# Attention and two expert layers on one core: for 24 pairs of heads the products with values are made two pairs at a time

## The chip, the cores and the metric

The kernel runs on one core of a Trainium2 chip. The metric is the device time of one execution in microseconds (us). Besides the DMA queues the core has five engines that run side by side, each through its own instructions in program order: TensorE (PE in the profile; PEld is its loading of stationary operands), VectorE (DVE), ScalarE (ACT), GpSimd (POOL) and SyncE (SP), which here issues nearly all DMAs.

## The reference, cut to what matters

```python
scores = scale * np.matmul(q, k.transpose(0, 1, 3, 2))        # (2, 8, 576, 576), head_dim 64
kth = np.partition(scores, -32, axis=-1)[..., -32:-31]
scores = np.where(scores >= kth, scores, -1e9)
attn = np.exp(scores - scores.max(-1, keepdims=True))
attn = attn / (attn.sum(-1, keepdims=True) + 1e-09)
attn_out = np.matmul(attn, v)                                 # then (1152, 512), heads side by side
out = sum(p[:, e:e+1] * (relu(x @ w1[e]) @ w2[e]) for e in range(4))      # w1 (4, 512, 1024)
return np.maximum(np.maximum(out @ m1, out @ m2), out @ m3) @ m_out        # 512 -> 768 -> 512
```

## The kernel before, in words

The 1152 rows are cut into 9 tiles of 128 and the 8 heads into 4 pairs, so there are 36 units of attention, numbered n = 0 to 35; the code calls such a unit a `Pair` (128 rows, two heads). Tile 4 (`MIXED`) has 64 rows of either batch; its units are n = 16, 18, 20 and 21. The program is written slot by slot: unit n begins at slot 8n, and tables (`LOOSE`, `BOTH`, `THIRD`) say at which slot each of its steps is emitted. For the units spoken of here these steps are, counted from slot 8n:

- -4 and 0: `scores` (two heads j), TensorE into two PSUM banks each (L418, L423), ScalarE copies to `s` (L430). `s` of head 0 has a ring of 5 buffers, of head 1 one of 4.
- 0 to 11: `topk`, VectorE takes the largest 8 four times (L443) and strikes them out (L445); then ScalarE or VectorE make the masked exponentials `p` with their sums (L457 to L471).
- 14: `trans_p`, TensorE turns `p` (four 128x128 blocks of each head, L489, and one of the two ends, L494) and ScalarE copies to `pt` (L492, L497). 14 and 15: `guard` (L502), `recip` on VectorE (L508), 16: `spread` on ScalarE, `rb` (L512), one buffer.
- 17: `pv`, the products with values into one bank `psv`: the block diagonal `v_last` over the full array (L531, two instructions for each such product), then for four row blocks and two heads a product over half of the array's columns (L534, 16 instructions; a unit of tile 4 does both parts for either batch in turn). 17: `trans_r`, TensorE turns `rb` (L517), ScalarE copies to `r` two slots later (L519).
- 20 and 21: `norm` on VectorE (L541, `psv` times `r`), `split_x`: ScalarE rounds to `xh` (L554), GpSimd takes the rest `xl` (L555).

Between the slots a planner emits products of the expert layers (L680 to L682 in three terms of a split product, L765 to L842 for unsplit ones) until the charged TensorE time (`pe(...)`) reaches that charged to VectorE (`dve(...)`). Their weights come over SP into `raw` (L212, 5 buffers), ScalarE rounds them (`whi`, L271), GpSimd or VectorE take the rest (`wlo`, L277); ScalarE applies Relu to a finished bank (`h`, L822) and VectorE takes the rest (L824). After unit 35 only the products and the conversion of the second layer's 64-bit weights are left (`wide_load` L222 into the buffers of `s`).

`v` has five buffers and `v_last` six for the eight pieces (batch, pair of heads); the load of piece (1, 2), L345 and L349, is emitted one slot behind the products of unit 19, and takes the buffer of `v` that unit 18 reads last.

Of the kernel before, what the change touches and what calls it, by code (L numbers as in the profile page):

```python
# [10 lines left out]
F32 = mybir.dt.float32  # L11
# [3 lines left out]
AF = mybir.ActivationFunctionType  # L15
ALU = mybir.AluOpType
# [12 lines left out]
S1 = 4  # L29
# [15 lines left out]
LOOSE = dict(stag=4, new=1, scores=-4, at=(14, 14), pv=17, rec=15, lag=2, sum=0)  # L45

EARLY = 7

ALONE_FROM, ALONE_STEP = -8, 4
LOAD, LOAD_FULL = 11, 9  # L50
SHARE, AHEAD = (1.0, 1.0, 1.0), 6
AHEAD_S = 5
# [8 lines left out]
def kernel(  # L61
# [14 lines left out]
    nc = tc.nc  # L76
    B, HP, D, _, S = k.shape
    NT, DM = out.shape
    E = gates.shape[2]
    P = 128  # L80
# [3 lines left out]
    NR = S // P  # L84
    TAIL = S - NR * P
# [5 lines left out]
    MIXED = 4  # L91
# [17 lines left out]
    const = ctx.enter_context(tc.tile_pool(name="const", bufs=1))  # L109
    kv = ctx.enter_context(tc.tile_pool(name="kv", bufs=2))  # L110
    qp = ctx.enter_context(tc.tile_pool(name="qp", bufs=2))
    at = ctx.enter_context(tc.tile_pool(name="at", bufs=2))
# [7 lines left out]
    ident = const.tile([P, P], F32, name="ident")  # L120
# [12 lines left out]
    def pe(n):  # L133
        clock["pe"] += n / 2400.0

    def bank(name):
        return pg.tile([P, 512], F32, tag="g", name=name)
# [169 lines left out]
    kraw, kT, vt, qraw, qT = {}, {}, {}, {}, {}  # L307
# [11 lines left out]
            nc.sync.dma_start(out=kfull[rows(n), heads], in_=k[0, hp][:, heads])  # L319
            between()  # L320

    v_last = [const.tile([P, P], F32, name="v_last%d" % i) for i in range(6)]
    for x in v_last:
        nc.gpsimd.memset(x, 0.0)

# [71 lines left out]
    class Pair:  # L397
        def __init__(self, n):
            self.n = n
            self.c, self.hp, self.t = pairs[n]  # L400
            self.s, self.w, self.m, self.nb = {}, {}, {}, {}
            self.p = self.rs = None
            self.pt = {}

            self.did = set()

            self.on_pool = [n in ON_POOL[j] for j in range(2)]
            self.on_act = [n in ON_ACT[j] for j in range(2)]
# [74 lines left out]
        def trans_p(self, part):  # L483
            assert {("p", j) for j in range(2) if part in (j, 2)} <= self.did
            ps = bank("psp")
            pe(260 * (NR if part < 2 else 1))
            if part < 2:
                for r in range(NR):
                    nc.tensor.transpose(ps[:, r * P:(r + 1) * P], self.p[:, part, part * TAIL + r * P:part * TAIL + (r + 1) * P], ident)  # L489
                d = at.tile([P, NR, P], F32, tag="pt%d" % part, bufs=1, name="pt")  # L490
                self.pt[part] = d
                return lambda: [nc.scalar.activation(out=d, in_=ps.rearrange("p (r n) -> p r n", r=NR), func=AF.Copy),  # L492
                                self.did.add(("pt", part))]
            nc.tensor.transpose(ps[:, 0:P], self.p.rearrange("p j s -> p (j s)")[:, NR * P:NR * P + 2 * TAIL], ident)  # L494
            d = at.tile([P, P], F32, tag="pt2", name="pt4")
            self.pt[2] = d
            return lambda: [nc.scalar.activation(out=d, in_=ps[:, 0:P], func=AF.Copy), self.did.add(("pt", 2))]  # L497
# [10 lines left out]
            nc.vector.reciprocal(out=self.rr, in_=self.rs)  # L508

        def spread(self):  # L510
            self.rb = at.tile([P, 2, D], F32, tag="rb", bufs=1, name="rb")
            nc.scalar.activation(out=self.rb, in_=self.rr.unsqueeze(2).to_broadcast([P, 2, D]), func=AF.Copy)  # L512

        def trans_r(self):
            ps = bank("psr")
            pe(260)
            nc.tensor.transpose(ps[:, 0:P], self.rb.rearrange("p a d -> p (a d)"), ident)  # L517
            self.r = at.tile([P, P], F32, tag="r", name="r")
            return lambda: [nc.scalar.activation(out=self.r, in_=ps[:, 0:P], func=AF.Copy), self.did.add("r")]  # L519

        def pv(self):
            assert {("pt", i) for i in range(3)} <= self.did
            ps = bank("psv")
            pe((NR + 1) * 512)
            if self.t == MIXED:
                parts = [(0, slice(0, TAIL)), (1, slice(TAIL, P))]
            else:
                parts = [(0 if self.t < MIXED else 1, slice(0, P))]
            for b, cols in parts:
                vs, last = vt[b, self.hp]  # L530
                nc.tensor.matmul(ps[:, cols], lhsT=last, rhs=self.pt[2][:, cols], start=True, stop=False)  # L531
                for r in range(NR):
                    for j in range(2):
                        nc.tensor.matmul(ps[j * D:(j + 1) * D, cols], lhsT=vs[:, j * NR + r, :],  # L534
                                         rhs=self.pt[j][:, r, cols], start=False, stop=r == NR - 1)
            self.x = ps

        def norm(self):
            assert "r" in self.did
            self.xt = xfull[:, self.hp, :] if [self.t] in STAGES else at.tile([P, P], F32, tag="xt", bufs=2 + WAITING, name="xt")  # L540
            nc.vector.tensor_tensor(out=self.xt, in0=self.x[:, 0:P], in1=self.r, op=ALU.mult)  # L541

        def split_x(self):
            if not room(self.t):
# [12 lines left out]
    def attention():  # L557

        NP = len(pairs)
        prs = {}  # L560
        later, between = {}, {}

        def options(n):
            return TIGHT if n == HP - 1 else SECOND if n == 2 * HP - 1 else MIDDLE if n in (HP - 2, 2 * HP - 3, 2 * HP - 2) else FIRST if n < 2 * HP else THIRD if n == 3 * HP - 1 else BOTH if n in ON_ACT[1] else LOOSE

        def at_slot(s, f, *a):
            later.setdefault(s, []).append((f, a))
# [3 lines left out]
        for n, (c, hp, t) in enumerate(pairs):  # L571
# [8 lines left out]
            elif n:  # L580
                o = options(max(0, n - 2))
                at_slot(max(8 * n + options(n)["scores"] - LOAD_FULL, 8 * (n - 2) + o["scores"] + o["stag"] + 1), load_full, n)
        free = {"k": -99, "q": -99}
        for key, n in first_use.items():
            if key[0] == "v":
                continue
            s0 = 8 * n
            load, split = (load_k, split_k) if key[0] == "k" else (load_q, split_q)
            at = max(s0 + options(n)["scores"] - (SPLIT_K if key[0] == "k" else SPLIT_Q), free[key[0]] + 2)
            if key[0] == "k" and key[1] and key[2]:  # L590

                at = max(at, 8 * pairs.index((MIXED, key[2] - 1, MIXED)) + options(n)["scores"] + options(n)["stag"] + (1 if key[2] == HP - 1 else 4))
# [3 lines left out]
        for n, (c, hp, t) in enumerate(pairs):  # L596
            s0 = 8 * n
            prs[n] = Pair(n)
            pr = prs[n]
            o = options(n)  # L600

            def two(s, f, *a, lag=o["lag"]):
                at_slot(s, lambda: at_slot(s + lag, f(*a)))
            for j in range(2):
                b0 = s0 + o["stag"] * j
                two(b0 + o["scores"], pr.scores, j, lag=o.get("lag_s", o["lag"]))
                for i in range(7):
                    if o["new"]:
                        later.setdefault(b0 + i, []).insert(0, (pr.topk, (j, i)))
                    else:  # L610
                        at_slot(b0 + i, pr.topk, j, i)
                at_slot(b0 + 2, pr.negate, j)
                at_slot(b0 + 5, pr.exp, j)
                late = o.get("late", MASK_LATE) * pr.on_act[j]
                two(b0 + 7 + late, pr.mask, j, lag=o["sum"] if n < EARLY else 3)
                two(s0 + o["at"][j] if "at" in o else b0 + o["trans"] + late + (late > 0), pr.trans_p, j, lag=o.get("lag_t", o["lag"]))
            two(s0 + o["at"][1] if "at" in o else s0 + o["stag"] + o["trans"], pr.trans_p, 2, lag=o.get("lag_t", o["lag"]))
            at_slot(s0 + o.get("guard", o["rec"] - 1), pr.guard)
            at_slot(s0 + o["rec"], pr.recip)
            at_slot(s0 + o.get("spread", o["rec"] + 1), pr.spread)  # L620
            at_slot(s0 + o["pv"], pr.pv)
            two(s0 + o.get("turn", o["rec"] + 2), pr.trans_r)
            end = max(o["pv"], o["rec"] + 2) + o["lag"]
            if "norm" in o:
                between.setdefault(s0 + o["norm"], []).append((pr.norm, ()))
            else:
                at_slot(s0 + end + 1, pr.norm)
            two(s0 + o.get("split", end + 2), pr.split_x)
        last = {}
        for n, p in enumerate(pairs):  # L630
            o = options(n)
            last[p[0:2]] = 8 * n + o.get("last", max(o["pv"], o["rec"] + 2) + 2 * o["lag"] + 2)
        for n in range(len(alone)):
            at_slot(ALONE_FROM + ALONE_STEP * n, load_alone, n + 1)
        end = max(last.values()) + 1
        s = min(later)
        while s <= end:
            todo = later.pop(s, [])
            i = 0
            while i < len(todo):  # L640
                f, a = todo[i]
# [45 lines left out]
    def begun(ps, wt, xs, N, parts):  # L687

        for f in range(2):
            for a in parts:  # L690

                product(spread(ps[:, f * N:(f + 1) * N], xs[0][a]), [w[:, a, f * P:(f + 1) * P] for w in wt], [x[a] for x in xs], f == a == 0, False)
            yield True
# [386 lines left out]
```

## Time and profile before

| what | us |
|---|---|
| median of 3 runs (lowest, highest) | 752.18 (751.92, 754.55) |
| the profiled execution, its span | 750.64, 748.7 |
| PE busy | 727.5 (97%) |
| PEld busy | 644.9 (86%) |
| DVE busy | 605.3 (81%) |
| ACT busy | 494.1 (66%) |
| POOL busy | 458.2 (61%) |

The span is the time from the first to the last instruction of the profiled execution; 1.94 us of its time lie around it. A matmul is recorded from its start to a modelled end, and matmuls overlap in the array, so what one costs in a stream is read from start to start, not from its duration. The granted clock of TensorE was 1.00 in nearly every stretch.

### The profile page before, as it was taken

The page shows a single profiled execution, that of the slowest core. Times are in us where ns is not written, and L with a number is a line of the kernel's source. Part 1 is how long each engine was busy: PE and PEld are TensorE (multiplying, and loading weights), DVE is VectorE, ACT ScalarE, POOL GpSimd, SP SyncE. Part 2 cuts the span into 40 slices and gives each one's busy share as a digit, 9 for nine tenths or more (in the row PEclk, how much of TensorE's full clock was granted, in tenths as well). Part 3 has the DMA queues.
Part 4 walks back from the last instruction along what each step waited for, and adds up shares of the span by engine and source line. Part 5 has one row for each costly group of instructions (what it writes and reads, how often), then busy time and mean ns, then how long its engine had stood idle before and what let it go on. Part 6 is the DMA issues. An engine that isn't in the chain of part 4 may idle for free.

```text
span 748.7 us, 13553 instructions
## 1 busy us (share of the span) xinstructions
PE 727.5 (97%) x4678; PEld 644.9 (86%) x4678; DVE 605.3 (81%) x1160; ACT 494.1 (66%) x1127; POOL 458.2 (61%) x401
## 2 busy tenths in 40 slices
PE   6899999999999999999999999999999999999998
PEld 3586789888999999898989877999888899999996
DVE  6999989989999899999999958999999643233341
ACT  4668889899987787788796665666555533432531
POOL 2514778689979787697775226678676733442520
PEclk9999999999999999999999999999999999999999
DMA  7684555545637464445433759888688351443501
GB/s 218 185 263 161 154 172 171 154 127 166 188 121 217 114 183 127 146 138 165 132 115 105 281 187 355 248 253 284 222 267 270 135 195 69 157 167 99 196 2 43
DMA packets 56484, 130.14 MB, mean 174 GB/s; under 512 B 9760, under 2 KB 23328, under 8 KB 56416
## 3 DMA queue, kind: packets, MB, share of 16 engines
q1 hardware_dynamic: 48064, 120.69, 51.6%
q10 hardware_dynamic: 8352, 8.59, 3.2%
q8 instruction: 37, 0.61, 0.3%
q14 instruction: 31, 0.25, 0.1%
HBM read 120.60 MB, written 8.65 MB: 173 GB/s over the span
## 4 chain that ended last, share of the span: by engine, by line
PE 65%; DVE 17%; ACT 10%; issue 4%; POOL 3%; DMA 1%; SPq 0%; ACTq 0%; POOLq 0%
PE ps L680 15%; PE ps L682 15%; PE ps L681 15%; DVE m L443 8%; DVE work L445 6%; ACT whi L271 3%; PE psv L534 2%; PE ps L842 2%; POOL wlo L277 2%; PE pss L423 2%; PE psp L489 2%; PE pso L680 2%; PE psa L765 2%; PE pso L681 2%; PE pso L682 2%
## 5 line engine op out<-in xcount | busy, mean ns | idle before, releaser
L277 POOL TENSOR_TENSOR wlo<-raw,whi 128x512 fp32r<-128x512 f32 x228 | 302.9, 1356 | 110.9 <-ACT whi L271 108.3
L271 ACT ACTIVATE whi<-raw 128x1024 fp32r<-128x1024 f32 x148 | 152.6, 1056 | 32.6 <-POOL narrow L248 14.7
L680 PE MATMUL ps<-xl,whi 128*128 128x256 f32 (+1 forms) x520 | 161.0, 310 | 0.3 <-POOL xl L555 0.3
L682 PE MATMUL ps<-xh,wlo 128*128 128x256 f32 (+1 forms) x520 | 157.7, 303 | 0.0
L681 PE MATMUL ps<-xh,whi 128*128 128x256 f32 (+1 forms) x520 | 157.6, 303 | 0.0
L443 DVE MAX8 m<-work 128x8 f32<-128x576 f32 x216 | 155.3, 746 | 0.1
L445 DVE MATCH_REPLACE8 work<-m,work 128x576 f32<-128x576 f32 x144 | 106.9, 743 | 0.0
L680 PEld LDWEIGHTS ps<-xl,whi 128*128 128x128 f32 x520 | 98.6, 190 | 1.7 <-POOL xl L555 0.6
L277 DVE TENSOR_TENSOR wlo<-raw,whi 128x1024 fp32r<-128x1024 f32 x34 | 53.4, 1570 | 56.8 <-ACT whi L271 44.8
L681 PEld LDWEIGHTS ps<-xh,whi 128*128 128x128 f32 x520 | 98.0, 188 | 1.2 <-issue 0.7
L682 PEld LDWEIGHTS ps<-xh,wlo 128*128 128x128 f32 x520 | 97.8, 188 | 0.0
L248 POOL TENSOR_TENSOR narrow<-narrow,raw 128x256 int32<-128x256 int32 x48 | 44.6, 929 | 40.1 <-DVE narrow L245 14.6
L680 PE MATMUL ps<-wlo,h 128*128 128x512 f32 x160 | 65.3, 408 | 0.6 <-POOL wlo L277 0.6
L682 PE MATMUL ps<-whi,h 128*128 128x512 f32 x160 | 63.0, 394 | 1.3 <-POOL h L817 1.3
L681 PE MATMUL ps<-whi,h 128*128 128x512 f32 x160 | 62.7, 392 | 0.0
L430 ACT ACTIVATE s<-pss 128x288 f32<-128x288 f32 x144 | 51.3, 400 | 12.0 <-PE pss L418 11.3
L443 DVE MAX8 m<-s 128x8 f32<-128x576 f32 x72 | 53.9, 748 | 4.0 <-ACT s L430 4.0
L445 DVE MATCH_REPLACE8 work<-m,s 128x576 f32<-128x576 f32 x72 | 53.4, 742 | 0.0
L682 PE MATMUL ps<-x2h,wlo 128*128 128x384 f32 x144 | 48.5, 336 | 0.0
L681 PE MATMUL ps<-x2h,whi 128*128 128x384 f32 x144 | 48.3, 335 | 0.0
L680 PE MATMUL ps<-x2l,whi 128*128 128x384 f32 x144 | 48.2, 335 | 0.0
L947 DVE TENSOR_TENSOR tm<-ps,tm 128x384 f32<-128x384 f32 x36 | 19.9, 555 | 34.1 <-PE ps L682 32.1
(118 smaller groups left out, 1617.7 us busy)
## 6 DMA issues: line engine op xcount, KB each, us to landing
raw<-in_w_dram SPq DMA_DIRECT2D x112, 512.0 KB, 4.2
raw<-narrow SPq DMA_DIRECT2D x36, 512.0 KB, 3.9
whole<-in_w_dram SPq DMA_DIRECT2D x30, 512.0 KB, 5.5
raw<-in_m_dram SPq DMA_DIRECT2D x36, 256.0 KB, 5.1
narrow<-narrow ACTq DMA_DIRECT2D x48, 128.0 KB, 4.5
kraw<-in_k_dram SPq DMA_DIRECT2D x16, 288.0 KB, 4.5
qraw<-in_q_dram SPq DMA_DIRECT2D x48, 64.0 KB, 3.8
raw<-in_mo_dram SPq DMA_DIRECT2D x12, 256.0 KB, 4.1
```

Of the source, the lines that this page charges most:

```text
L248: nc.gpsimd.tensor_tensor(out=out.bitcast(I32), in0=out.bitcast(I32), in1=last, op=ALU.add)
L271: nc.scalar.activation(out=hi, in_=raw, func=AF.Copy)
L277: on.tensor_tensor(out=lo[:, x], in0=raw[:, x], in1=hi[:, x].bitcast(F32), op=ALU.subtract)
L423: nc.tensor.matmul(ps[:, 0:SH], lhsT=l, rhs=r, start=i == 0, stop=i == len(mm) - 1)
L430: nc.scalar.activation(out=s[:, h, :], in_=halves[h][:, 0:SH], func=AF.Copy)
L443: nc.vector.max(m[:, 8 * r:8 * r + 8], src)
L445: nc.vector.match_replace(out=self.w[j], in_to_replace=m[:, 8 * r:8 * r + 8], in_values=src, imm_value=NEG)
L489: nc.tensor.transpose(ps[:, r * P:(r + 1) * P], self.p[:, part, part * TAIL + r * P:part * TAIL + (r + 1) * P], ident)
L680: nc.tensor.matmul(ps, lhsT=lh, rhs=rl, start=first, stop=False)
L681: nc.tensor.matmul(ps, lhsT=lh, rhs=rh, start=False, stop=False)
L682: nc.tensor.matmul(ps, lhsT=ll, rhs=rh, start=False, stop=last)
L947: nc.vector.tensor_tensor(out=tm[:, g], in0=ps, in1=tm[:, g], op=ALU.max)
```

## The change

For twelve units (`HELD`), all even, `pv`, `trans_r`, `norm` and `split_x` are not emitted at their own slots but together with those of the next unit, at that unit's slots: first the block diagonals of both (L531), then all half-array products of both (L534), in two column blocks of one PSUM bank, then both transposes of reciprocals in one bank, two copies to `r`, two `norm`, two `split_x`. All other steps stay at their slots. A held unit's `pt` of the two heads lies in the rings of `s` instead of in the single `pt` buffers; `rb` gets two buffers, `v_last` five instead of six. For a unit of tile 4 both block diagonals come ahead of the half-array products too, held or not.

```diff
+HELD = (8, 12, 14, 16, 18, 22, 24, 26, 28, 30, 32, 34)
-    v_last = [const.tile([P, P], F32, name="v_last%d" % i) for i in range(6)]
+    v_last = [const.tile([P, P], F32, name="v_last%d" % i) for i in range(5)]
...
-                d = at.tile([P, NR, P], F32, tag="pt%d" % part, bufs=1, name="pt")
+                if self.held:
+                    d = at.tile([P, NR, P], F32, tag="s%d" % part, bufs=(AHEAD_S, S1)[part], name="pt")
+                else:
+                    d = at.tile([P, NR, P], F32, tag="pt%d" % part, bufs=1, name="pt")
...
-            self.rb = at.tile([P, 2, D], F32, tag="rb", bufs=1, name="rb")
+            self.rb = at.tile([P, 2, D], F32, tag="rb", name="rb")
...
+        def trans_r(self, *held):
+            both = [*held, self]
             ps = bank("psr")
+            for i, x in enumerate(both):
+                pe(260)
+                nc.tensor.transpose(ps[:, i * P:(i + 1) * P], x.rb.rearrange("p a d -> p (a d)"), ident)
+                x.r = at.tile([P, P], F32, tag="r", name="r")
+            def copy():
+                for i, x in enumerate(both):
+                    nc.scalar.activation(out=x.r, in_=ps[:, i * P:(i + 1) * P], func=AF.Copy)
...
+        def pv(self, *held):
+            both = [*held, self]
             ps = bank("psv")
...
+            pe((NR + 1) * 512 * len(both))
...
+            for i, (x, b, cols) in enumerate(uses):
+                nc.tensor.matmul(x.x[:, cols], lhsT=vt[b, x.hp][1], rhs=x.pt[2][:, cols], start=not i, stop=False)
+            for i, (x, b, cols) in enumerate(uses):
                 for r in range(NR):
                     for j in range(2):
+                        nc.tensor.matmul(x.x[j * D:(j + 1) * D, cols], lhsT=vt[b, x.hp][0][:, j * NR + r, :],
+                                         rhs=x.pt[j][:, r, cols], start=False, stop=i == len(uses) - 1 and r == NR - 1)
...
+            if pr.held:
+                continue
+            both = [prs[n - 1], pr] if n - 1 in HELD else [pr]
+            at_slot(s0 + o["pv"], pr.pv, *both[:-1])
+            two(s0 + o.get("turn", o["rec"] + 2), pr.trans_r, *both[:-1])
             end = max(o["pv"], o["rec"] + 2) + o["lag"]
+            for x in both:
...
+                    at_slot(s0 + end + 1, x.norm)
+                two(s0 + o.get("split", end + 2), x.split_x)
...
         for n, p in enumerate(pairs):
+            n += n in HELD
```

## Rows read from the trace of the kernel before

**Rows 1.** The chain that ended last, shares of the span by engine.
```profile
PE 65%; DVE 17%; ACT 10%; issue 4%; POOL 3%; DMA 1%; SPq 0%; ACTq 0%; POOLq 0%
```

**Rows 2.** TensorE in order of time: start, length, instruction, [idle ahead <- releaser]; unit 35.
```profile
440.78 0.49 PE L531 MATMUL psv<-pt,v_last 128*128 128x128 f32 x2 [1.22 <-ACT pt L497]
```

**Rows 3.** Busy time by stretch: PE, PEld, DVE, ACT, POOL, granted clock, DMA.
```profile
240.00:338.00 98.00, 97.10 (x770) 88.03 (x769) 92.27 (x199) 78.84 (x191) 78.26 (x69) 1.00 0.49 146
338.00:433.00 95.00, 94.90 (x696) 84.15 (x695) 93.44 (x203) 70.96 (x180) 57.96 (x54) 1.00 0.51 165
```

**Rows 4.** The chain in order of time, 262 to 345: start, length, what.
```profile
317.63 0.17 ACT r L519
...
320.75 0.16 ACT xh L554
...
322.51 0.69 DVE h L824
...
338.39 0.53 PE pss L423 x2
```

**Rows 5.** The same chain at the end of attention, 424 to 446.
```profile
433.41 0.45 PE psp L489 x4
...
438.41 0.21 DVE xt L541
...
439.08 0.18 DVE rr L508
```

**Rows 6.** ScalarE in order of time, unit 34.
```profile
433.55 0.31 ACT L512 ACTIVATE rb<-rr 128x128 f32<-128x128 f32 x1 [3.08 <-DVE rr L508]
433.89 1.08 ACT L492 ACTIVATE pt<-psp 128x512 f32<-128x512 f32 x2
```

**Rows 7.** TensorE in order of time, unit 23.
```profile
301.25 0.38 PE L531 MATMUL psv<-pt,v_last 128*128 128x128 f32 x2
301.57 1.09 PE L534 MATMUL psv<-pt,vt 128*64 128x128 f32 x16
302.59 0.33 PE L517 MATMUL psr<-ident,rb 128*128 128x128 f32 x1
302.68 0.36 PE L680 MATMUL ps<-xl,whi 128*128 128x256 f32 x1
302.88 0.28 PE L681 MATMUL ps<-xh,whi 128*128 128x256 f32 x1
302.99 0.28 PE L682 MATMUL ps<-xh,wlo 128*128 128x256 f32 x1
```

**Rows 8.** The half-array products of unit 23 in flight at 302.10.
```profile
301.84 0.50 PE L534 MATMUL psv<-pt,vt 128*64 128x128 f32 x6
```

**Rows 9.** Instructions on `psv`: duration ns min/median/max, first and last start.
```profile
L534 PE MATMUL psv<-pt,vt x640: 222/273/477, 25.6 to 442.0; 128*64 128x128 f32 x128, 128*64 128x64 f32 x32
```

**Rows 10.** Waits, 240 to 433: who for whom, total, times, longest.
```profile
DVE h L824 <- ACT h L822: 6.3, 7, 1.7
PE psv L531 <- ACT pt L497: 0.9, 1, 0.9
```

**Rows 11.** ScalarE in order of time, near units 19, 23 and 33.
```profile
258.01 1.07 ACT L271 ACTIVATE whi<-raw 128x1024 fp32r<-128x1024 f32 x1
...
305.24 0.27 ACT L519 ACTIVATE r<-psr 128x128 f32<-128x128 f32 x1
...
427.33 0.28 ACT L519 ACTIVATE r<-psr 128x128 f32<-128x128 f32 x1 [0.52 <-PE psr L517]
```

**Rows 12.** SP's queue in order of time, from the load of piece (1, 2).
```profile
241.04 0.34 SPq L345 DMA_DIRECT2D vt<-in_v_dram  x1
...
242.65 5.77 SPq L212 DMA_DIRECT2D raw<-in_w_dram  x2
```

**Rows 13.** TensorE in order of time, unit 19.
```profile
250.73 0.38 PE L531 MATMUL psv<-pt,v_last 128*128 128x128 f32 x2
```

**Rows 14.** DMA issues, page part 6: count, KB, median us to landing.
```profile
raw<-in_w_dram SPq DMA_DIRECT2D x112, 512.0 KB, 4.2
```

More of the change, by code (lines that the diff above doesn't have):

```diff
@@ L405, in __init__ @@
             self.did = set()
+            self.held = n in HELD
             self.on_pool = [n in ON_POOL[j] for j in range(2)]
@@ L510, in spread @@
         def spread(self):
-            self.rb = at.tile([P, 2, D], F32, tag="rb", bufs=1, name="rb")
+            self.rb = at.tile([P, 2, D], F32, tag="rb", name="rb")
             nc.scalar.activation(out=self.rb, in_=self.rr.unsqueeze(2).to_broadcast([P, 2, D]), func=AF.Copy)
-        def trans_r(self):
+        def trans_r(self, *held):
+            both = [*held, self]
             ps = bank("psr")
[L516 to L519, printed above, removed]
@@ L521, in pv @@
-        def pv(self):
-            assert {("pt", i) for i in range(3)} <= self.did
-            ps = bank("psv")
[L524 to L531, printed above, removed]
+            for i, x in enumerate(both):
+                pe(260)
+                nc.tensor.transpose(ps[:, i * P:(i + 1) * P], x.rb.rearrange("p a d -> p (a d)"), ident)
+                x.r = at.tile([P, P], F32, tag="r", name="r")
@@ new lines, in copy @@
+            def copy():
+                for i, x in enumerate(both):
+                    nc.scalar.activation(out=x.r, in_=ps[:, i * P:(i + 1) * P], func=AF.Copy)
+                    x.did.add("r")
+            return copy
+        def pv(self, *held):
+            both = [*held, self]
+            ps = bank("psv")
+            for i, x in enumerate(both):
+                assert {("pt", a) for a in range(3)} <= x.did
+                x.x = ps[:, i * P:(i + 1) * P]
+            pe((NR + 1) * 512 * len(both))
+            uses = []
+            for x in both:
+                if x.t == MIXED:
+                    uses += [(x, 0, slice(0, TAIL)), (x, 1, slice(TAIL, P))]
+                else:
+                    uses += [(x, 0 if x.t < MIXED else 1, slice(0, P))]
+            for i, (x, b, cols) in enumerate(uses):
+                nc.tensor.matmul(x.x[:, cols], lhsT=vt[b, x.hp][1], rhs=x.pt[2][:, cols], start=not i, stop=False)
+            for i, (x, b, cols) in enumerate(uses):
@@ L532, in pv @@
                 for r in range(NR):
                     for j in range(2):
-                        nc.tensor.matmul(ps[j * D:(j + 1) * D, cols], lhsT=vs[:, j * NR + r, :],
-                                         rhs=self.pt[j][:, r, cols], start=False, stop=r == NR - 1)
-            self.x = ps
+                        nc.tensor.matmul(x.x[j * D:(j + 1) * D, cols], lhsT=vt[b, x.hp][0][:, j * NR + r, :],
+                                         rhs=x.pt[j][:, r, cols], start=False, stop=i == len(uses) - 1 and r == NR - 1)
@@ L540, in norm @@
             self.xt = xfull[:, self.hp, :] if [self.t] in STAGES else at.tile([P, P], F32, tag="xt", bufs=2 + WAITING, name="xt")
-            nc.vector.tensor_tensor(out=self.xt, in0=self.x[:, 0:P], in1=self.r, op=ALU.mult)
+            nc.vector.tensor_tensor(out=self.xt, in0=self.x, in1=self.r, op=ALU.mult)
         def split_x(self):
@@ L620, in attention @@
             at_slot(s0 + o.get("spread", o["rec"] + 1), pr.spread)
-            at_slot(s0 + o["pv"], pr.pv)
-            two(s0 + o.get("turn", o["rec"] + 2), pr.trans_r)
-            end = max(o["pv"], o["rec"] + 2) + o["lag"]
[L624 to L628, printed above, removed]
+            if pr.held:
[3 more added lines that the diff above has]
+            two(s0 + o.get("turn", o["rec"] + 2), pr.trans_r, *both[:-1])
+            end = max(o["pv"], o["rec"] + 2) + o["lag"]
+            for x in both:
+                if "norm" in o:
+                    between.setdefault(s0 + o["norm"], []).append((x.norm, ()))
+                else:
+                    at_slot(s0 + end + 1, x.norm)
+                two(s0 + o.get("split", end + 2), x.split_x)
         last = {}
         for n, p in enumerate(pairs):
+            n += n in HELD
             o = options(n)
```

## The prediction

> **What bounds the kernel now.** I read first the chain that ended last. TensorE has 65% of it, VectorE 17%, ScalarE 10% [rows 1]. That mean hides two regimes. Behind the products with values of unit 35 at 440.78 [rows 2] nothing but expert products is left on TensorE: 748.7 - 440.8 = 307.9 us, 41% of the span. So of TensorE's 65% only some 24%, about 180 us, lie in the 440 us of attention, and more than half of the chain there runs over other engines. The change acts in attention alone; what it saves counts only where TensorE is the one that is late.
>
> Next I read busy times by stretch. From 240 to 338 TensorE is busy 97.1 of 98 us, VectorE 92.3; from 338 to 433 they are 94.9 and 93.4 of 95 [rows 3]. The two are nearly level, so the shares don't say which one is late. The chain in order of time does: from 262 on it alternates between VectorE's top-k and ScalarE, such as 317.63 (`r`), 320.75 (`xh`), then VectorE's `h` at 322.51, and goes over to TensorE at 338.39 [rows 4]. There it stays until the transposes of unit 34 at 433.41 [rows 5]. Even that hand-over is all but a tie: ScalarE had been waiting 3.08 us for VectorE's reciprocal, made `rb` at 433.55 and began its copy of `pt` at 433.89 [rows 6]. The reader is to see a TensorE that never rests, with a VectorE beside it that would take over within some tenths of a us if TensorE got faster.
>
> **What a merged block saves on TensorE.** Unit 23 shows one block whole [rows 7]. It starts at 301.25; the reciprocal's transpose starts at 302.59; the next products start at 302.68, 302.88 and 302.99, where the step 302.68 to 302.88 is 0.20 instead of the 0.11 of the following one. So a block takes 302.88 - 301.25 - 0.11 = 1.52 us of TensorE's stream. In its middle six half-array instructions, three pairs, cover 0.50 us [rows 8]. One lasts 0.27 (median) [rows 9], so the third pair starts 0.23 behind the first and a pair costs 0.11. All eight pairs at that rate are 0.88 us, but from the first half-array instruction to the transpose it is 302.59 - 301.57 = 1.02: 0.14 is lost there. The two block-diagonal instructions take 0.32 where two at 0.11 would be 0.22: 0.10 is lost. The transpose and the step behind it take 0.09 + 0.20, where two at 0.11 would be 0.22: 0.07 is lost. I add 0.10 + 0.14 + 0.07 = 0.31 us for going in and out of the half-array form and the transpose. A merged block pays this once for two units: 12 x 0.31 = 3.7 us. Four units of tile 4 go in and out twice; by the new order they do so once. No row here isolates that; the bounds are nothing and 4 x 0.24 (the 0.10 and 0.14 above) = 1.0; I take 0.5. TensorE's work falls by about 4.2 us.
>
> One rule of the Trainium skill bears on the price: its page TensorEngine Tiling (Array Packing), section Key Properties, says that changing the tiling mode drains the engine, and TensorE: Matmul & The Clock Gate, section Step-by-step, has the last column need about 128 more cycles. At 2.4 GHz this is 53 ns, an estimate from the page; two changes for each of 12 blocks would be 1.3 us. The rows above show more, and I use the rows.
>
> **Where that saving lands.** (a) In 338 to 433, where TensorE carries the chain, the blocks of 27, 29, 31 and 33 lie: 4 x 0.31 = 1.2 at most. The copy at 433.89 could have begun right behind `rb`, 433.55 + 0.31 = 433.86 [rows 6]: if VectorE gains nothing on the way, 0.03 of it is reached; if it follows, all. I take -0.4 (0 to -1.2). Elsewhere in attention the saving turns into TensorE's waiting: nothing, or at the far end all 4.2 (rival B).
>
> (b) A unit's copy to `r` and its rounding to `xh` move eight slots, out of the even periods into the odd ones. VectorE waited 7 times for ScalarE's Relu in 240 to 433, 6.3 us together [rows 10]. In the even unit 24 both copies lay in the chain ahead of such a wait, 0.17 + 0.16 [rows 4]; that goes. In the odd unit 23 one `r` of 0.27 lies at 305.24 [rows 11] shortly ahead of another wait; that doubles. Some three waits gain 0.3, two lose 0.3: -0.3 (-1 to +1). The copies cost the same in number; what covers them is ScalarE's wait for the reciprocal, 3.08 at unit 34, and without that cover one costs 0.27.
>
> (c) At the end of attention `norm` and `xh` of unit 34 stand in the chain ahead of unit 35's reciprocal, from 438.41 to 439.08 [rows 5]. Merged, they come behind it, and of these 0.67 us only `guard` itself, about 0.2, remains. -0.5 (0 to -0.7).
>
> (d) The last block is then that of 34 and 35, 1.52 - 0.31 = 1.2 longer behind 440.78. But the planner charges a unit's `pv` and transpose (2560 + 260)/2400 = 1.18 us, and fills what left the even slot with expert products of about that length, which need not come later. +0.1 (-0.5 to +1.2).
>
> (e) SP is moved against a later release. Piece (1, 2) of `v` takes the buffer of piece (0, 1), whose last reader is unit 18. SP issued that load at 241.04 and two weight pieces behind it from 242.65 [rows 12]. Unit 18 now goes with unit 19, at 250.73 [rows 13]; three block diagonals and the first quarter of the half-array products put the release at about 252. The weights behind it then go out at 252 + 1.6 (the 241.04 to 242.65 of three issues) = 253.6 and land 4.2 later [rows 14], 257.8, against their rounding on ScalarE at 258.01 [rows 11]. That just holds. If DMAs bunch and it lands 1.5 us later, ScalarE stands, and behind it the softmax of unit 20. I take +0.2 (0 to +1.5). The load of (1, 1) waits for unit 16, whose new place still lies ahead of that load's slot, and that of (1, 3) for unit 20, which is not held: nothing for both.
>
> (f) The other buffers: `pt` of a held unit sits in a ring of `s` from slot 14 to 25; the allocation that takes it comes four or five steps on, at slot 32 or later. That is 7 slots of cover, some 10 us, so nothing; without cover a score copy would wait. The second `rb` and fewer banks can only help. `norm` moves with its length. Nothing is taken for these.
>
> Sum: -0.4 - 0.3 - 0.5 + 0.1 + 0.2 = -0.9. On the profiled execution 750.64 gives 749.7; the median shown is 1.54 above that execution, 752.18, and the forecast for a median is 752.18 - 0.9 = 751.3. One can tell no change from a change at about 0.5%, 3.8 us here: 748.4 to 755.9.
>
> **Rivals.**
>
> *A: about level, 751.3* (748.5 to 753), as summed: chance 0.47. For it speaks the near tie of [rows 6], against it that TensorE has no rest in any stretch.
>
> *B: TensorE is the bound after all.* Being faster it lets ScalarE and VectorE run ahead, and the whole 4.2 counts, with the wait of 0.9 at unit 24's products that a held unit no longer meets [rows 10] and (c): 752.2 - 4.2 - 0.9 - 0.5 = 746.6, or some 748 if a part is lost. For it: 97% busy, and VectorE's 6.3 us of waits leave it room to follow. Against it: the chain at 262 to 338. Chance 0.30.
>
> *C: ScalarE waits at `r`, slower.* ScalarE runs in order; its first copy to `r` now waits for the second transpose, behind a block that is 1.2 longer. At unit 33 the copy already waited 0.52 for TensorE [rows 11], so there all 1.2 would be added. At every one of the 12 blocks, and all passed on to VectorE, that is 14.4 at most. But at unit 23 the copy met no wait [rows 11], and the products that move ahead give most of the length back; I price it at three such blocks, 3 x 1.2 = 3.6, and 755.8. It decides where ScalarE has less than 1.2 us in hand at `r` and VectorE nothing to do meanwhile. Chance 0.15.
>
> *D: SP's late release* (e) at its full price, and a second piece late behind it: 752.2 + 1.5 to 3 = 754 to 755. Chance 0.08.
>
> The Trainium skill has a rule against the change as such: TensorEngine Tiling (Array Packing), section PSUM Bottleneck, says that a faster TensorE leaves the evacuation of PSUM as it is, which may then bound. By it (a) is nothing and the result 751.7; the ScalarE rows in the chain agree with it before 338, not behind.
>
> **How the numbers follow.** The likeliest is A, 751.3. Faster by over 0.5%: nearly all of B and a little of A, 0.31. Slower by over 0.5%: most of C and a little of D, 0.16. Same: the rest, 0.53. For 8 in 10 the range reaches to B's 746 and to just past C's 755.8.
>
> **What would show it.** Right: the span from one block's start to the products behind it grows from 1.52 to about 2.7 for two units; unit 35's block starts some 0.5 earlier; VectorE's waits for `h` stay near 6 us in sum; TensorE's waits grow. B would show as unit 35's block at 437 or earlier. C would show as waits of ScalarE at `r` of over 1 us in the odd units, with VectorE's waits behind them; D as a wait of `whi` for a DMA near 258. The prediction is wrong if the emission of the expert products, shifted by the planner, moves ScalarE's Relus against the top-k by more than the waits shown.

## The result, and the profile after

The changed kernel takes 757.0 us (median of 12 executions, 755.39 to 762.84), the kernel before beside it 751.68 (12, 750.72 to 754.55): a ratio of 1.0085 [1.0066, 1.0103]. It is slower by more than the half per cent that a measurement can tell, and lies outside the range of 746 to 756. The profiled execution took 755.39 with a span of 753.6, against 750.64 and 748.7: 4.75 us more, at a granted clock of 1.000 in either. All comparisons below that speak of stretches are between profiled executions.

The saving on TensorE is there. Its instructions in order of time, the merged block of units 8 and 9 and the start of the last block; they answer to [rows 7] and [rows 2]:

```profile
130.61 0.61 PE L548 MATMUL psv<-pt,v_last 128*128 128x128 f32 x4
131.15 1.97 PE L552 MATMUL psv<-pt,vt 128*64 128x128 f32 x32
133.05 0.44 PE L524 MATMUL psr<-ident,rb 128*128 128x128 f32 x2
133.24 0.37 PE L702 MATMUL ps<-xl,whi 128*128 128x256 f32 x1
133.45 0.28 PE L703 MATMUL ps<-xh,whi 128*128 128x256 f32 x1
...
446.43 0.49 PE L548 MATMUL psv<-pt,v_last 128*128 128x128 f32 x2 [0.57 <-ACT pt L502]
```

From the block's start to the second product behind it, less the usual 0.12 of one such step, it is 133.45 - 130.61 - 0.12 = 2.72 us for two units, where [rows 7] give 2 x 1.52 = 3.04. So 0.32 is saved, as forecast (0.31). TensorE's busy time falls from 727.5 to 724.6. But the part of unit 35 in the last block starts at 446.43 instead of 440.78, 5.65 later. The shares of the chain that ended last show who holds the path now; TensorE has lost 7 points of [rows 1], VectorE and ScalarE have gained 3 each:

```profile
PE 58%; DVE 20%; ACT 13%; issue 3%; POOL 3%; DMA 2%; SPq 0%; ACTq 0%; POOLq 0%; DVEq 0%
```

The stretches of [rows 3] (PE, PEld, DVE, ACT, POOL, granted clock, DMA):

```profile
240.00:338.00 98.00, 95.98 (x768) 87.41 (x767) 93.83 (x204) 79.91 (x193) 78.22 (x69) 1.00 0.48 147
338.00:433.00 95.00, 92.22 (x684) 83.54 (x684) 92.11 (x196) 71.83 (x178) 61.53 (x56) 1.00 0.48 155
```

TensorE, which rested 1.0 of these 193 us, now rests 4.8. VectorE is about as busy as it was (185.9 against 185.7). So TensorE isn't the engine that got late by working more; it stands. Its longest waits in all of attention and ScalarE's two that bear on the rivals (who for whom, total, times, longest, 30 to 455), the kernel before first:

```profile
ACT r L519 <- PE psr L517: 8.5, 10, 1.9
ACT pt L492 <- PE psp L489: 6.4, 8, 1.6
...
PE ps L682 <- POOL h L817: 1.3, 1, 1.3
```
```profile
PE ps L704 <- POOL h L839: 4.6, 4, 1.7
PE psp L499 <- ACT raw L837: 1.9, 1, 1.9
...
ACT r L529 <- PE psr L524: 11.5, 9, 2.8
...
ACT pt L497 <- PE psp L491: 8.7, 8, 2.7
```

So TensorE's waits for GpSimd's `h` grew from 1.3 to 4.6 us, ScalarE's for TensorE's transposes of `p` from 6.4 to 8.7.

**Where the time goes.** The VectorE reciprocal of each unit (`rr`, one instruction a unit) marks how far attention has come. After minus before it is within 0.2 us up to unit 9, then +2.38 at unit 10; it hardly moves to unit 12, reaches +4.42 at unit 17, is +4.86 at 19, falls to +2.72 at 20, lies near 3.1 to 4.0 from 21 to 28, jumps to +5.14 at 29 and +6.33 at 31, and ends at +5.42 (439.08 against 444.50) at unit 35. Behind that some 0.7 comes back: of 5.65 us at the last block 4.9 are left at the end of the span. The loss comes in a few steps inside attention, the first and largest behind the first held unit, 8. VectorE's reciprocals of units 9 and 10, before and after:

```profile
124.64 0.16 DVE L508 RECIPROCAL rr<-rs 128x2 f32<-128x2 f32 x1
137.35 0.15 DVE L508 RECIPROCAL rr<-rs 128x2 f32<-128x2 f32 x1
```
```profile
124.61 0.15 DVE L513 RECIPROCAL rr<-rs 128x2 f32<-128x2 f32 x1
139.72 0.15 DVE L513 RECIPROCAL rr<-rs 128x2 f32<-128x2 f32 x1
```

This step can be read instruction by instruction. TensorE of before between unit 8's block and unit 9's transposes emits six products with `h` from 119.63, the scores, and twelve more products. The ninth of these, at 122.02, needs the rest of `h`, which GpSimd makes from 120.51 to 121.81; it just comes late enough:

```profile
119.63 0.40 PE L680 MATMUL ps<-wlo,h 128*128 128x512 f32 x1
...
121.02 0.29 PE L423 MATMUL pss<-kT,ql 128*128 128x288 f32 x1
...
122.02 0.40 PE L682 MATMUL ps<-whi,h 128*128 128x512 f32 x1
...
124.30 1.04 PE L489 MATMUL psp<-ident,p 128*128 128x128 f32 x8
```

The same stretch after, with the block gone from it (the first line is the eighth product, the second the ninth):

```profile
119.85 0.40 PE L703 MATMUL ps<-whi,h 128*128 128x512 f32 x1
121.94 0.50 PE L704 MATMUL ps<-whi,h 128*128 128x512 f32 x1 [1.69 <-POOL h L839]
...
122.96 0.29 PE L425 MATMUL pss<-kT,ql 128*128 128x288 f32 x1
...
126.22 1.03 PE L491 MATMUL psp<-ident,p 128*128 128x128 f32 x8
```

GpSimd makes that operand at its old time, first before and then after:

```profile
120.51 1.30 POOL L817 TENSOR_TENSOR h<-raw,h 128x512 fp32r<-128x512 f32 x1
```
```profile
120.60 1.28 POOL L839 TENSOR_TENSOR h<-raw,h 128x512 fp32r<-128x512 f32 x1
```

The planner has pulled six products of 0.23 us each, which stood behind unit 9's transposes (125.20 to 126.68 before), ahead of the scores at 122.96: six with `h` stood there, now twelve. They fill the 1.42 us of the block (116.71 to 118.13) almost exactly with 1.37. But the ninth comes to its turn at 120.08, and its operand isn't made: TensorE stands until 121.94, 1.86 later than the stream would have it. Unit 9's transposes come 1.92 late. What that does to ScalarE and VectorE, in rows of either engine, first before:

```profile
124.94 1.09 ACT L492 ACTIVATE pt<-psp 128x512 f32<-128x512 f32 x2 [1.04 <-PE psp L489]
...
130.91 0.70 ACT L430 ACTIVATE s<-pss 128x288 f32<-128x288 f32 x2
```
```profile
131.63 0.76 DVE L443 MAX8 m<-s 128x8 f32<-128x576 f32 x1 [0.50 <-ACT s L430]
...
132.97 0.27 DVE L541 TENSOR_TENSOR xt<-psv,r 128x128 f32<-128x128 f32 x1
133.24 0.69 DVE L824 SCALAR_TENSOR_TENSOR h<-ps,h 128x512 fp32r<-128x512 f32 x1
```

and after:

```profile
126.86 1.09 ACT L497 ACTIVATE pt<-psp 128x512 f32<-128x512 f32 x2 [2.73 <-PE psp L491]
...
132.83 0.69 ACT L432 ACTIVATE s<-pss 128x288 f32<-128x288 f32 x2
```
```profile
133.55 0.76 DVE L445 MAX8 m<-s 128x8 f32<-128x576 f32 x1 [1.55 <-ACT s L432]
...
135.22 0.49 DVE L558 TENSOR_TENSOR xt<-psv,r 128x128 f32<-128x128 f32 x2 [0.25 <-ACT r L529]
135.62 0.68 DVE L846 SCALAR_TENSOR_TENSOR h<-ps,h 128x512 fp32r<-128x512 f32 x1
```

ScalarE runs in order: it stands at the copy of unit 9's `pt` for 2.73 instead of 1.04, and its copy of unit 10's scores begins 1.92 later. VectorE's top-k of unit 10 begins 1.92 later; the double `norm` adds 0.22 (0.49 against 0.27) and its wait for `r` 0.25. Together 2.39: VectorE's `h` moves from 133.24 to 135.62, and unit 10's reciprocal by 2.38.

### The profile page after: what moved, and what is told of

It is laid out like the page before. It is cut to its first block, busy times and chain, and to the rows that moved or that the text cites. A ratio compares the mean times of both kernels' runs of the same rounds, so it can differ in the third digit from the quotient of the medians.

```text
span 753.6 us, 13575 instructions
## 1 busy us (share of the span) xinstructions
PE 724.6 (96%) x4678; PEld 643.5 (85%) x4678; DVE 606.1 (80%) x1160; ACT 494.1 (66%) x1127; POOL 458.6 (61%) x400
## 4 chain that ended last, share of the span: by engine, by line
PE 58%; DVE 20%; ACT 13%; issue 3%; POOL 3%; DMA 2%; SPq 0%; ACTq 0%; POOLq 0%; DVEq 0%
PE ps L704 13%; PE ps L702 13%; PE ps L703 13%; DVE m L445 9%; DVE work L447 8%; ACT whi L272 3%; PE psv L552 2%; PE ps L864 2%; ACT pt L497 2%; PE pso L702 2%; PE psa L787 2%; POOL wlo L278 2%; PE pso L703 2%; PE pso L704 2%; PE ps L823 1%
## 5 line engine op out<-in xcount | busy, mean ns | idle before, releaser
L278 POOL TENSOR_TENSOR wlo<-raw,whi 128x512 fp32r<-128x512 f32 x228 | 306.6, 1374 | 108.0 <-ACT whi L272 101.1
L278 DVE TENSOR_TENSOR wlo<-raw,whi 128x1024 fp32r<-128x1024 f32 x34 | 51.1, 1502 | 56.4 <-ACT whi L272 42.0
```

Of the source, the lines that this page charges most:

```text
L278: on.tensor_tensor(out=lo[:, x], in0=raw[:, x], in1=hi[:, x].bitcast(F32), op=ALU.subtract)
```

## The experiments

Theory, after this comparison: the time is lost because the planner's charge moved with the products (1.18 us of charged TensorE time for each held unit), so that expert products come earlier in the even slots and the attention's hand-over between TensorE, ScalarE and VectorE is displaced. Rivals: the longer block itself holds up `r` and VectorE (rival C of the prediction); the buffers, `pt` in the rings of `s` above all; TensorE's clock, because 10 of the 12 executions of the changed kernel have a mean granted clock of 0.991 to 0.998, where the kernel before has 0.997 or more in every execution beside these runs. Each group below shares its runs of the kernel before.

**The charge and the merge apart.** The change with a held unit's charge left at its old slot:

```diff
+            pe(260)
             for i, x in enumerate(both):
-                pe(260)
...
-            pe((NR + 1) * 512 * len(both))
+            pe((NR + 1) * 512)
...
             if pr.held:
+                at_slot(s0 + o["pv"], lambda: pe((NR + 1) * 512 + 260))
                 continue
```

> The merged kernel, but the planner is charged for a held unit's products and transpose at the unit's own slot, as before, and for its own alone at the next unit's: the expert products keep their old places among the slots. Theory 1 (the products that move ahead into the even slots meet operands that are not ready, and push ScalarE's later work back): the 5 to 6 us of loss go, and what the merged blocks save may show: 748 to 752. Theory 2 (the double block itself makes ScalarE and VectorE late): still 755 to 758. Theory 3 (buffers: pt in the rings of s, one v_last less, SP's later release): still 755 to 758.

Measured 753.7 (12, 751.96 to 764.58), 1.0041 [1.0021, 1.0061]. Five executions lie within 751.96 to 752.10 at clock 1.000, some 1.0 over the kernel before, the others from 753.7 up. By the medians half of the loss is gone, which lies between the ranges of theory 1 and theories 2 and 3; by the executions at clock 1.000 three quarters are gone (1.0 left of 3.8). In its trace unit 10's reciprocal is 0.38 late instead of 2.38, unit 35's 0.65 instead of 5.42.

The kernel before, nothing merged, its charges alone moved by one unit (the same for `pe(260)`):

```diff
-            pe((NR + 1) * 512)
+            pe((NR + 1) * 512 * (0 if self.n in HELD else 2 if self.n - 1 in HELD else 1))
```

> The kernel before, nothing merged, with the planner's charges alone shifted as the change shifts them (none at a held unit's slot, both at the next unit's). Theory 1: slower by 3 to 6 us, 755 to 758. Theories 2 and 3: within 1.5 us of the kernel before.

Measured 758.62 (4, 758.49 to 760.29), 1.0106 [1.0093, 1.0119]. No product with values has moved, no buffer has changed, and the kernel loses 7.6 us, more than the change itself. ScalarE at unit 9 reads as in the changed kernel, and the next line is VectorE at unit 10:

```profile
126.84 1.09 ACT L493 ACTIVATE pt<-psp 128x512 f32<-128x512 f32 x2 [2.73 <-PE psp L490]
```
```profile
133.54 0.76 DVE L444 MAX8 m<-s 128x8 f32<-128x576 f32 x1 [1.56 <-ACT s L431]
```

Here the block still stands ahead of the six pulled products. So these hold up the transposes by their own length, and the wait for GpSimd is only 0.20; the delay is the same. The other steps of the loss are there as well: the reciprocals are 2.16 late at unit 10, 4.03 at 17, 4.66 at 19, 2.82 at 20, 6.64 at 29, 9.20 at 31 and 8.29 at 35. So the shift alone follows the change within 0.7 us up to unit 27, the gain at unit 20 included, and loses more from 28 on.

**The merge, its two halves apart.** The change, but each unit's diagonal and half-array products in turn inside one block:

```diff
                 nc.tensor.matmul(x.x[:, cols], lhsT=vt[b, x.hp][1], rhs=x.pt[2][:, cols], start=not i, stop=False)
-            for i, (x, b, cols) in enumerate(uses):
                 for r in range(NR):
```

> The merged kernel, but in a block the block diagonal and half-array products of the first unit come ahead of those of the second, so that TensorE goes into the half-array form as often as before. If TensorE's time counts all the way, slower than the change by 12 x 0.24 = 2.9 us and some tenths for tile 4: 760. If attention is bound beside TensorE, within 1 us of the change: 756 to 758.

Measured 756.71 (4, 756.27 to 757.05; a fifth execution took 4033 us and is left out), 1.0075 [1.0062, 1.0088]. Without the joint stretch of half-array products it is as slow, so that stretch is not what costs. Against the change's two executions at clock 1.000 (755.39 and 755.48) it lies some 1.3 higher, and its unit 35 comes 1.4 later: about that much the joint stretch may be worth where TensorE is late. The two come from different groups of runs.

The kernel before with the changed buffers alone:

```diff
-    v_last = [const.tile([P, P], F32, name="v_last%d" % i) for i in range(6)]
+    v_last = [const.tile([P, P], F32, name="v_last%d" % i) for i in range(5)]
...
+                if self.n in HELD:
+                    d = at.tile([P, NR, P], F32, tag="s%d" % part, bufs=(AHEAD_S, S1)[part], name="pt")
+                else:
+                    d = at.tile([P, NR, P], F32, tag="pt%d" % part, bufs=1, name="pt")
...
-            self.rb = at.tile([P, 2, D], F32, tag="rb", bufs=1, name="rb")
+            self.rb = at.tile([P, 2, D], F32, tag="rb", name="rb")
```

> The kernel before with the buffers of the change alone: pt of the twelve units in the rings of s, two rb, five v_last; nothing merged or moved. Theories 1 and 2: within 1 us of the kernel before. Theory 3: slower by 3 us or more, 755.

Measured 750.88 (11, 750.52 to 752.68), 1.0001 [0.9993, 1.001]. The buffers by themselves cost nothing.

**The clock.** The change once more, for a second trace:

> The changed kernel once more, for its trace. Its executions spread from 755.4 to 762.8, those at a mean granted clock of 1.000 lie at 755.4, the others at 0.991 to 0.998. If this one falls below 1.000, the trace shows a stretch at 1.2 GHz and what TensorE did before it. Theory of the merged half-array stretch: it begins behind merged blocks. Theory of the waits: it begins behind a wait of TensorE of more than 1 us.

755.67 at a mean clock of 0.995. It shows what lowers the mean; the section on the hardware has its rows. And the last two edits together, one after the other on the old charges:

> Merged, charged at the old slots, and in a block the first unit's products ahead of the second's: TensorE saves next to nothing, the expert products stay where they were. If the long unbroken stretch of half-array products is what lowers the granted clock, its clock is 0.999 or more in every execution and it takes 752 to 753. If the waits do it, it spreads as the run with charges at the old slots did, 752 to 759.

Measured 753.2 (12, 753.05 to 760.05), 1.0039 [1.0016, 1.0061]. Eight executions lie within 753.05 to 753.42 at clock 1.000, four are at 0.997 to 0.998 and reach 760. I had expected every clock at 0.999 or above: a miss, so the lower clock doesn't come from the long stretch of half-array products. At clock 1.000 it lies some 1.7 over the kernel before of its group, the first experiment some 1.0: the joint stretch is again worth something, about 0.7.

**How a loss travels.** The change for unit 8 alone, `HELD = (8,)`:

> The change for one unit, 8, and no other. In the changed kernel the reciprocal of unit 10 comes 2.4 us later than before, and no other held unit is by then done. Theory 1: 1.5 to 2.5 us slower than before, 753. If later units make up for such a loss: within 1 us of the kernel before.

Measured 752.88 (12, 752.53 to 756.88), 1.0025 [1.0014, 1.0037]. Unit 10's reciprocal is 2.51 late, unit 17's 2.51, unit 23's 2.61, unit 35's 2.68. In 25 units VectorE and ScalarE make up nothing of it.

The kernel before with its charges moved the other way, the held unit charged double and the next one nothing:

```diff
-            pe((NR + 1) * 512)
+            pe((NR + 1) * 512 * (2 if self.n in HELD else 0 if self.n - 1 in HELD else 1))
```

> The kernel before with the charges shifted the other way: both units' at the held unit's slot, none at the next one's, so that expert products move behind the odd units' transposes instead of ahead of them. If it is the products ahead of the transposes that cost: within 1.5 us of the kernel before, 750 to 752.5. If any departure from the even order costs: slower by 3 us or more, 754 to 759.

Measured 760.2 (6, 757.22 to 765.86), 1.0132 [1.0099, 1.0164]. Part of it goes with a low clock; the one execution at clock 1.000 took 757.22. Products that come later cost about as much as products that come earlier, so it is not that expert products in the even slots are bad as such. But they cost elsewhere: unit 10's reciprocal is 0.54 early here, unit 19's 3.10 late, unit 25's 1.54, unit 28's 4.52 and unit 35's 5.20. The reading at unit 9 explains the step at unit 10, not every step; all that is shown for the rest is that either shift loses.

**Can the merge pay?** The change on the old charges, for unit 8 alone; for all held units but 8 and 18, where the first experiment's trace had its largest steps; and for the last six, where [rows 4] put TensorE on the chain:

```diff
-HELD = (8, 12, 14, 16, 18, 22, 24, 26, 28, 30, 32, 34)
+HELD = (8,)
...
+HELD = (12, 14, 16, 22, 24, 26, 28, 30, 32, 34)
...
+HELD = (24, 26, 28, 30, 32, 34)
```

> Unit 8 alone held, charged at its own slot. Held with the charge moved it cost 2.5 us at unit 10's reciprocal. Theory 1 (the charge): no more than 0.9 us is left, 751.5 to 752. Theory 2 (the merged block): 2.5 us again, 753 to 754.

> Merged and charged at the old slots, but units 8 and 18 are not held (ten are). With all twelve held in that way the reciprocals lost 0.76 us up to unit 11 and 1.6 us at units 18 and 19, and gained 1.7 at the rest. If each merge's effect stays in its own place, this is faster than before by some 1.5 us: 749.5. If every merge outside the planner's tuned order costs, it stays slower: 752 or more.

> Six units held, 24 to 34, charged at the old slots: the stretch in which TensorE carries the chain of the kernel before. If TensorE's saving counts there: faster than before by 1 to 1.9 us, 749.5 to 750.5. If VectorE and ScalarE bind as closely as the tie at unit 34 says: within 0.5 us of before.

Measured, in this order: 751.31 (11, 751.15 to 753.23), 1.0007 [0.9998, 1.0016]; 751.97 (11, 750.96 to 753.34), 1.0006 [0.9992, 1.002]; 751.28 (12, 750.56 to 760.18), 1.0012 [0.9991, 1.0034]. With unit 8 alone the transposes of unit 9 are back at 124.20, although a product still waits 1.19 for GpSimd's `h`, and the six products stand behind them again. The block itself still costs something in the trace: unit 10's reciprocal is 0.28 late, unit 12's 0.80, unit 35's 0.86, within the 0.9 that was expected; by the medians it is 0.26. Its ScalarE at unit 9 and VectorE at unit 10:

```profile
124.84 1.09 ACT L497 ACTIVATE pt<-psp 128x512 f32<-128x512 f32 x2 [0.99 <-PE psp L491]
```
```profile
131.53 0.76 DVE L445 MAX8 m<-s 128x8 f32<-128x576 f32 x1 [0.50 <-ACT s L432]
```

The run without 8 and 18 missed: I had hoped for 1.5 us below the kernel before. The reciprocal of unit 17 comes 1.37 earlier there, and 1.7 is lost again by unit 19, although 18 is no longer held; at unit 35 0.30 is left. At unit 18 TensorE is the late one: ScalarE's Relu at 236.47 waits 2.49 for a product of the expert layers, where in the kernel before it waits 1.51 and runs at 236.33, and `rb` and `pt` of unit 18 stand behind it.

The last six are level, as the second of the two expectations had it, but not for its reason. Unit 33's reciprocal comes 0.92 earlier and unit 35's 0.87, so merging does gain there. The last block gives it back. The part of unit 35 in it and the products behind it, which begin at 440.78 [rows 2] and 442.39 in the kernel before:

```profile
439.91 0.49 PE L548 MATMUL psv<-pt,v_last 128*128 128x128 f32 x2 [0.86 <-ACT pt L502]
...
442.50 1.06 PE L824 MATMUL ps<-xfull,whole 128*128 128x128 f32 x8
```

The part of unit 35 begins 0.87 earlier, the products behind it 0.11 later, and the span is 748.7 in both. Units 24 to 32 merged on the old charges, without 34, was not run; 0.7 to 0.9 us faster is an estimate from the reciprocals of units 34 and 35 in this trace, too little to tell from no change.

**The same cell without the merge.** The kernel before with the charge of unit 8 alone moved:

> The kernel before, nothing merged, with the charge of unit 8 alone moved to unit 9's slot: the fourth corner beside unit 8 merged with the charge moved, merged with the old charge, and the kernel before. Theory 1: the transposes of unit 9 start about 2 us later, ScalarE stands 2.7 us ahead of their copy, and the time is 1.5 to 2.5 us over the kernel before, 752.5 to 753.5. Theory 2: within 0.5 us of the kernel before.

Measured 752.74 (11, 752.55 to 753.97), 1.0018 [1.0008, 1.0028], 1.4 by the medians. Unit 9's transposes start at 126.79, ScalarE stands 2.02 at `pt` instead of the 2.7 expected, unit 10's reciprocal is 2.74 late; no product waits for GpSimd's `h` there. In this trace unit 8's reciprocal is already 1.50 late, ahead of the moved charge, so the size of the loss is better read from the median than from the 2.74. So for unit 8 all four cells are measured: neither, 1; the merge alone, 1.0007; the shift alone, 1.0018; both, 1.0025. Most of it is the shift.

## Why the prediction was wrong

The saving in the block was right: 0.32 against 0.31 us, by the route of [rows 7 to 9]. TensorE was 2.9 us less busy, where 4.2 were summed. Tile 4 is not what fell short: unit 20, which isn't held, takes 2.26 us from its block's start to the second product behind it before (264.12 to 266.38) and 1.97 after (268.12 to 270.09), 0.29 less, where the bound for a unit was 0.24. But not every merged block saves 0.32; that of units 28 and 29 stands 0.17 between its two block diagonals, for unit 29's `pt`. That a faster TensorE would hand on little was right for the time. (a) At unit 34 ScalarE copies `pt` at 439.71, behind `rb` at 439.42:

```profile
439.42 0.31 ACT L517 ACTIVATE rb<-rr 128x128 f32<-128x128 f32 x1 [3.08 <-DVE rr L513]
439.71 1.08 ACT L497 ACTIVATE pt<-psp 128x512 f32<-128x512 f32 x2
```

That is 0.29 behind it instead of 0.34 in [rows 6], while the wait for VectorE is 3.08 in both. So at this hand-over 0.05 was gained, as (a) had it for a VectorE that gains nothing. What TensorE's saving gives on the way there the changed kernel can't show, because the shift makes all of it late; the last six merged on the old charges can, with 0.92 at unit 33, in which (b) has its part; (a) took 0.4 and allowed 1.2. Rival B, all of 4.2 us counted, falls with the level results of the merge on old charges.

(b) VectorE's waits for ScalarE's Relu went from 6.3 to 5.7 us in 240 to 433 [rows 10]; -0.3 was forecast, and -0.6 is what the view shows. (c) From unit 34's reciprocal to unit 35's it is 444.50 - 439.23 = 5.27 us against 5.72 before: -0.45, where I took -0.5. (e) SP did stand longer behind its late release (the load of (1, 2) at 256.09 instead of 241.04 [rows 12]), and the next in the row from 260.04 to 269.33. No `whi` waited for a DMA there; +0.2 was too much, and rival D did not come. (f) The buffers cost nothing, as the run with them alone shows.

**The step that failed is (d)**, in the words "the planner charges a unit's `pv` and transpose (2560 + 260)/2400 = 1.18 us, and fills what left the even slot with expert products of about that length, which need not come later". The first half is what happened, to 0.05 us at unit 8. But I asked what this does for the last block alone, and gave it +0.1. There it was sound: the products behind the last block begin 6.64 later (449.03 against 442.39), 0.99 more than the part of unit 35 in that block, and 4.9 are left at the end. For the other eleven blocks I gave it nothing and asked only what the longer block does in the odd slot. The filling has a price of its own: what is pulled forward stands in front of unit 9's transposes, and in the changed kernel it needs an operand that another engine makes at its old time. Moving the charge alone, with no product of attention moved, costs 7.6 us (1.0106). The last sentence of the prediction named "the emission of the expert products, shifted by the planner", but as something that moves ScalarE's Relus, and gave it neither price nor chance. VectorE's waits for the Relu fell in 240 to 433 and rose from 11.6 to 13.4 us in 30 to 455, so they are the smaller part. The late piece, where I read it, is ScalarE's copy of `pt`, behind TensorE's transposes.

Rival C, forecast at 755.8, came near the time by another road. ScalarE's waits at `r` grew from 8.5 to 11.5 us. The 0.25 for `r` in the 2.39 at unit 10 is not the longer block's: VectorE waits the same 0.25 there when the charges alone move. And the merge on old charges for unit 8 has the same long block and costs 0.8 us in its trace and 0.3 by the medians, so the block is the smaller part there. Later it may have one: the chain that ended last runs over VectorE and ScalarE from 338 to 391 now, where [rows 4] had TensorE's, and behind that one passage goes over a merged block, `r` and VectorE (start, length, what):

```profile
338.50 1.32 DVE m L445 x2
...
408.42 0.45 PE psv L548 x4
408.87 1.90 PE psv L552 x32
410.77 0.38 PE psr L524 x2
411.17 0.45 ACT r L529 x2
...
411.80 0.74 DVE m L445
```

What that passage costs no run measures by itself.

What the two halves are worth together is read from three medians over the kernel before of their group: shift alone +7.6, shift and merge +5.3, merge alone +2.7 (its executions at clock 1.000 mostly +1.0). They don't add: on top of the shift the merge gives some 2.3 us back, and without it it costs a little. That it gives back because the shift has made TensorE late is likely and not shown. Of the 5.3 us, 4.75 are seen in the profiled execution at full clock. The rest goes along with executions of a lower mean clock; that the clock causes it is not shown.

Open are three things beside it. Why shifts in either direction cost at units 13 to 19 and 28 to 31; only the step at unit 10 was read instruction by instruction. Whether displaced TensorE instructions alone, or the order of ScalarE's copies that the planner displaces with them, carry most of the loss; no run separates the two. And what makes three of the twelve executions of the changed kernel 762 us; none of them has a trace. No version that was run beats the kernel before; the best are level with it.

## What to carry to other kernels

When a step is moved in a program whose gaps a planner fills, its charge moves too, and the filling is a change of its own: try the charge without the move and the move without the charge before pricing either. Ask of each filler that comes earlier whether its operands do, and which in-order engine stands behind it. Here, with TensorE and VectorE within some per cent of one another, a saving of 0.3 us a block bought nothing that the time shows, while the displacement of some 2 us at unit 8 was paid at once and, 25 units on, not made up.

## What the runs showed of the hardware

One thing I had not expected. TensorE's granted clock fell to its lower level, 1.2 of 2.4 GHz, inside a dense stream. From the second trace of the changed kernel, by stretches (the columns of [rows 3]):

```profile
184.00:188.00 4.00, 2.08 (x18) 1.84 (x17) 4.00 (x11) 4.00 (x10) 2.50 (x3) 1.00 0.78 273
188.00:192.00 4.00, 4.00 (x23) 4.00 (x22) 3.77 (x8) 3.97 (x10) 4.00 (x5) 0.57 0.69 220
...
383.00:386.30 3.30, 3.30 (x28) 2.97 (x25) 3.30 (x7) 2.59 (x10) 0.73 (x1) 0.50 0.00 0
```

and its TensorE at the beginning of either:

```profile
186.90 0.33 PE L499 MATMUL psp<-ident,p 128*128 128x128 f32 x1 [1.92 <-ACT raw L837]
...
381.09 0.49 PE L548 MATMUL psv<-pt,v_last 128*128 128x128 f32 x2 [1.41 <-ACT pt L497]
...
382.16 2.99 PE L552 MATMUL psv<-pt,vt 128*64 128x128 f32 x32
```

Each stretch comes shortly behind a wait of TensorE, 1.92 and 1.41 us long, and 32 half-array products take 2.99 us instead of 1.97. In the trace of the profiled execution the same two waits are 1.90 and 1.39, and the clock stays at 1.00 through both. So such a wait can be followed by half clock and need not be. The execution with the two stretches took 755.67 against 755.39, so two such stretches can pass at little cost. In the trace of the charges moved the other way a third stretch, 447.0 to 450.4 at 0.50, stands behind a wait of 1.55. The executions with a low mean clock are the slower ones on the whole (755.98 to 762.84 against 755.39 and 755.48 in the changed kernel), but the clock doesn't order them: 0.997 goes with 757.03 and with 762.63.
